# Attention and gated feed-forward on one core: one of two half-precision remainders moved from VectorE to GpSimd

## The chip, the cores and the metric

One core of a Trainium2 chip runs the whole program. The metric is the device time of one launch in microseconds (us); 1269.29 is the median of three runs before the change. The core has five engines with a queue of instructions each, worked off in order: TensorE (PE, whose weight loads appear as PEld), VectorE (DVE), ScalarE (ACT), GpSimd (POOL) and SyncE (SP, which only issues DMAs here).

## The reference

Block-causal attention over 8 batches of 8 heads, 576 positions, 64 dimensions, and behind it a feed-forward layer with a gate:

```python
scores = q @ k.T / 8                      # 64 x 64 blocks; a query sees its own and earlier blocks
attn = softmax(scores, masked)
x = (attn @ v) laid out as (8 * 576, 512)
h = x @ w_in                              # 512 -> 2048
out = (h * erf(softplus(h))) @ w_out      # 2048 -> 512
```

All inputs and outputs are 32-bit floats.

## The kernel before

Matrix products keep near 32-bit accuracy by splitting an operand into a high half in 16-bit floats and a low half, the remainder: `ph` is the rounded value, `pl` the value minus `ph`. A product is then three 16-bit matmuls (high x high, low x high, high x low).

**Attention.** A loop runs over the 64 heads `n`. In each turn the steps of several heads are merged: the loads of head n+3 (`load_qk`: two DMAs issued on GpSimd's queue, L383 and L385, one on SP's, then two GpSimd subtractions, L388 and L389, which make the low halves of keys and queries), the row maxima of head n+2 (`maxes`: matmuls L400, VectorE reductions L403 and L428), the probabilities of head n (`probs`) and, for every second n, the product with the values for heads n-2 and n-1 (`pv`: 42 matmuls of L495, then the row sums L518). Every fourth turn `normalise` scales two results and splits them (L578 on ScalarE, L579 on GpSimd) and stores them to DRAM (L580, issued on GpSimd's queue).

`probs` keeps the probabilities of one head in two column groups: part 0 with 832 columns, part 1 with 768. ScalarE writes exponentials (L451) into a 32-bit staging tile for each part (`p32_0`, `p32_1`, one buffer each). When a part is complete, `split` makes the two halves: ScalarE casts (L462), and an engine subtracts (L463). This happens for heads 24 to 63 only, thus 40 times for each part; the first 24 heads (batches 0 to 2) use the 32-bit values as they are. The last two steps of `probs` in a turn are the last two blocks of part 1, and `split(1)` behind them; so the low half of part 1 is made when the next turn has begun. For an odd head that turn is one that runs `pv`, whose 12th matmul is the first that reads the odd head's low half of part 1.

**Feed-forward.** In the same loop `moe1` feeds in units of the feed-forward layer on tokens whose attention is finished: 256 tokens by 256 of the 2048 features. A unit is 24 matmuls up (L190) into a PSUM bank `h`, of which there are two in the loop; the gate; and, three units later (`LAG = 3`), 12 matmuls down (L199). The gate is a chain that goes from engine to engine:

```python
# ScalarE L159, L160, L161: tanh of a scaled h, and two squares -> r0, r1 (SBUF)
nc.vector.scalar_tensor_tensor(out=r0, in0=r0, scalar=c3, in1=r0, op0=ALU.add, op1=ALU.mult)     # L162
nc.vector.scalar_tensor_tensor(out=r0, in0=r1, scalar=c4, in1=r0, op0=ALU.add, op1=ALU.mult)     # L163
nc.vector.scalar_tensor_tensor(out=r0, in0=r0, scalar=c5, in1=r0, op0=ALU.add, op1=ALU.mult)     # L164
nc.vector.scalar_tensor_tensor(out=r0, in0=r0, scalar=fin, in1=flat, op0=ALU.add, op1=ALU.mult)  # L165, flat is h in PSUM
nc.scalar.copy(gh, r0)                                                                            # L166
nc.gpsimd.tensor_tensor(out=gl, in0=r0, in1=gh, op=ALU.subtract)                                  # L167
```

After L165 the bank `h` is free for the unit after the next. When the heads are done, the remaining units run alone.

The order on each queue is set by a scheduler of the language, which replays the merged program with costs of its own and gives every engine its list; on the chip each list is worked off in order, and semaphores hold an instruction until its inputs are there.

Of the kernel before, what the change touches and what calls it, by code (L numbers as in the profile page):

```python
# [14 lines left out]
ALU = mybir.AluOpType  # L15
# [8 lines left out]
def f32(ap):  # L24
    return ap.bitcast(F32)
# [7 lines left out]
def tile_attention_moe(ctx: ExitStack, tc: tile.TileContext, qk, v, w, maskrows, sels, out):  # L33
    nc = tc.nc
# [259 lines left out]
    with tc.tile_pool(name="apool", bufs=2) as apool, tc.tile_pool(name="spool", bufs=1) as spool, \  # L294
# [14 lines left out]
        def bank(name):  # L309

            turn.append(0)
            k = len(turn) % 8 if not loaded else 0
            if k in (2, 5):
                return ps_h.tile([P, 512], F32, tag="h", name=name)
            if k in (3,):
                return ps_o.tile([P, 512], F32, tag="o", name=name)
            return ps_a.tile([P, 512], F32, tag="a", name=name)
# [55 lines left out]
        def part(n, i):  # L373

            return qks[n % NB][:, i * S : (i + 1) * S]
# [61 lines left out]
        def probs(n, out):  # L437

            K = D + 5
            klh, qhl, kh, qh = [part(n, i) for i in range(4)]  # L440

            def one(j, q0, w_, o):
                kk = min(P, S - j * P)
                ks = slice(j * P, j * P + kk)
                s = bank(f"t{j}_{n}_{q0}")
                nc.tensor.matmul(s[:kk, :w_], lhsT=kh[:K, ks], rhs=qh[:K, q0 : q0 + w_], start=True, stop=False)  # L446
                nc.tensor.matmul(s[:kk, :w_], lhsT=klh[:, ks], rhs=qhl[:, q0 : q0 + w_], start=False, stop=True)  # L447
                skip = max(0, starts[j] - q0)
                part, c = offs[j]
                c += q0 + skip - starts[j]  # L450
                nc.scalar.activation(p32s[part][:kk, c : c + w_ - skip], s[:kk, skip:w_], AF.Exp, scale=SCALE)  # L451

            pps = [apool.tile([P, 2, m], F16, tag=f"p{i}", name=f"p{i}_{n}", bufs=3) for i, m in enumerate(PN)]
            whole = n < B32 * H
            p32s = [f32(p.rearrange("p a b -> p (a b)")) for p in pps] if whole else pstage

            def split(part):
                if whole:
                    out.append((p32s[part],))
                    return  # L460
                ph, pl = pps[part][:, 0, :], pps[part][:, 1, :]
                nc.scalar.copy(ph, p32s[part])  # L462
                nc.vector.tensor_tensor(out=pl, in0=p32s[part], in1=ph, op=ALU.subtract)  # L463
                out.append((ph, pl))

            return [lambda: one(0, 0, 288, 0), lambda: one(0, 288, 288, 0), lambda: one(3, 320, 256, 0),
                    lambda: (one(4, 320, 256, 0), split(0)), lambda: one(1, 128, 448, 0),
                    lambda: (one(2, 256, 320, 0), split(1))]

        def pv(qd, pp, prs, V, usb, rs):  # L470
# [269 lines left out]
```

## Time and profile before

| | us |
|---|---|
| median of three runs (lowest, highest) | 1269.29 (1268.83, 1272.76) |
| the profiled execution | 1269.5 |
| its span, first to last instruction | 1267.5 |
| busy PE, DVE, ACT, POOL | 1174.1, 899.5, 778.0, 521.3 |
| L463 on VectorE, both parts: first and last start | 352.0, 1048.5 |
| L463, part 0 and part 1: busy | 44.2, 39.7 (40 instructions each) |

The page of the profile gives busy times of each engine, groups of instructions by source line with the idle time ahead of them and what ended it, and the chain of work that ended last. Matmuls are pipelined, and the busy time of PE contains this overlap. Beside the page stand answers of the trace for a stretch of time: the instructions in order with start and duration in us, and sums of what each engine waited for.

### The profile page before, as it was taken

The numbers are of one execution on the slowest core, as the hardware profiler recorded it, in microseconds if no ns is written. First come the engines' busy times: TensorE is split into PE (matmuls) and PEld (weight loads), VectorE is DVE, ScalarE is ACT, GpSimd is POOL, SyncE is SP. The second block draws the span as 40 slices with busy tenths as digits, with TensorE's granted clock in tenths as the row PEclk, the third lists the DMA queues.
The fourth block names the chain that finished last, engine by engine and source line by source line (L and its number), as shares of the span: only waits on it lengthen the run. The fifth ranks groups of instructions, "written<-read, shape, count | busy, mean of one in ns | idle before, by whom it ended". The sixth has DMA issues, their size and how long they took to land.

```text
span 1267.5 us, 23446 instructions
## 1 busy us (share of the span) xinstructions
PE 1174.1 (93%) x9018; PEld 812.4 (64%) x9018; DVE 899.5 (71%) x1601; ACT 778.0 (61%) x1555; POOL 521.3 (41%) x485
## 2 busy tenths in 40 slices
PE   5698798989999999999999999999999999999996
PEld 3465465566666666667667676766667766666563
DVE  4587698888677777887768777778777755464554
ACT  2465575667565666666666666665766765555543
POOL 6355454536443343545434453535444313212211
PEclk9777799999999999999999999999999999999999
DMA  9987568654444455354444554454444221121111
GB/s 235 221 211 191 140 186 196 168 131 114 111 120 112 120 120 126 98 141 118 100 115 117 122 124 116 116 125 118 109 126 116 58 68 58 54 83 35 59 58 50
DMA packets 95740, 151.72 MB, mean 120 GB/s; under 512 B 7738, under 2 KB 44922, under 8 KB 95630
## 3 DMA queue, kind: packets, MB, share of 16 engines
q1 hardware_dynamic: 69840, 93.34, 25.3%
q0 software_dynamic: 25120, 56.66, 22.2%
q8 instruction: 71, 1.16, 0.4%
q10 hardware_dynamic: 670, 0.23, 0.1%
q14 instruction: 39, 0.32, 0.1%
HBM read 121.66 MB, written 28.31 MB: 118 GB/s over the span
## 4 chain that ended last, share of the span: by engine, by line
PE 37%; DVE 30%; ACT 17%; DMA 8%; issue 5%; POOL 2%; ACTq 0%; DVEq 0%; SPq 0%; POOLq 0%
PE m_h L190 12%; PE o L199 11%; DVE m_r L163 6%; DVE m_r L162 5%; DVE m_r L164 5%; DVE m_r L165 4%; ACT m_r L159 4%; ACT m_r L160 4%; ACT m_r L161 4%; PE u L495 4%; DMA qk<-qk 2%; PE t L446 2%; DVE mx L403 2%; PE s L400 2%; DMA qk<-mt 2%
## 5 line engine op out<-in xcount | busy, mean ns | idle before, releaser
L190 PE MATMUL m_h<-xh,w 128*128 128x256 f16 x2304 | 477.2, 276 | 25.6 <-DVE m_r L165 18.5
L190 PEld LDWEIGHTS <-w 128*128 128x128 f16 x3456 | 328.0, 99 | 164.2 <-issue 33.7
L167 POOL TENSOR_TENSOR m_gl<-m_r,m_gh 128x512 f16<-128x512 f32 x144 | 175.6, 1220 | 423.5 <-ACT m_gh L166 365.2
L199 PE MATMUL o<-w,m_gh 128*128 128x512 f16 x1152 | 335.4, 383 | 12.2 <-DVE pt L240 8.6
L190 PE MATMUL m_h<-xl,w 128*128 128x256 f16 x1152 | 317.1, 275 | 0.3 <-DMA xl<-x_d 0.3
L162 DVE SCALAR_TENSOR_TENSOR m_r<-m_r 128x512 f32<-128x512 f32 x144 | 118.8, 825 | 189.8 <-ACT m_r L161 172.8
L403 DVE TENSOR_REDUCE mx<-s 64x1 f32<-64x288 f32 (+4 forms) x384 | 174.4, 469 | 83.8 <-PE s L400 82.6
L451 ACT ACTIVATE p<-t 128x288 f32<-128x288 f32 (+4 forms) x384 | 144.8, 384 | 99.5 <-PE t L447 89.0
L166 ACT CAST m_gh<-m_r 128x512 f16<-128x512 f32 x144 | 88.8, 617 | 188.6 <-DVE m_r L165 188.1
L199 PE MATMUL o<-w,m_gl 128*128 128x512 f16 x576 | 203.6, 383 | 0.3 <-POOL m_gl L167 0.3
L446 PE MATMUL t<-qk 69*128 69x288 f32 (+4 forms) x384 | 168.4, 439 | 11.2 <-DMA qk<-mt 8.0
L400 PE MATMUL s<-qk 68*64 68x288 f32 (+3 forms) x384 | 151.3, 425 | 27.0 <-DMA qk<-qk 21.9
L159 ACT ACTIVATE m_r<-m_h,c,bs 128x512 f32<-128x512 f32 (+3 forms) x192 | 124.3, 666 | 57.4 <-PE m_h L190 55.1
L388 POOL TENSOR_TENSOR qk<-st,qk 64x576 fp32r<-64x576 f32 x64 | 96.9, 1514 | 116.7 <-DMA qk<-qk 113.9
L199 PEld LDWEIGHTS <-m_gh 128*128 128x128 f16 x1152 | 100.5, 99 | 68.0 <-issue 17.3
L163 DVE SCALAR_TENSOR_TENSOR m_r<-m_r,m_r 128x512 f32<-128x512 f32 x144 | 121.0, 840 | 2.8
L447 PE MATMUL t<-qk 128*128 128x288 f32 (+4 forms) x384 | 120.4, 314 | 0.0
L164 DVE SCALAR_TENSOR_TENSOR m_r<-m_r 128x512 f32<-128x512 f32 x144 | 113.3, 787 | 2.4
L389 POOL TENSOR_TENSOR qk<-st,qk 64x576 fp32r<-64x576 f32 x64 | 99.3, 1552 | 35.9 <-DMA qk<-qk 28.1
L463 DVE TENSOR_TENSOR p<-p,p 128x832 f16<-128x832 f32 x80 | 84.0, 1050 | 34.8 <-ACT p L462 34.8
L161 ACT ACTIVATE m_r<-m_r,c 128x512 f32<-128x512 f32 x144 | 103.7, 720 | 2.8 <-ACT m_r L160 1.0
L160 ACT ACTIVATE m_r<-m_r,c 128x512 f32<-128x512 f32 x144 | 103.7, 720 | 1.7
(99 smaller groups left out, 1457.9 us busy)
## 6 DMA issues: line engine op xcount, KB each, us to landing
qk<-qk POOLq DMA_DIRECT2D x64, 432.0 KB, 5.0
st<-qk SPq DMA_DIRECT2D x64, 288.0 KB
qk<-qk POOLq DMA_DIRECT2D x64, 288.0 KB, 5.3
raw<-w SPq DMA_DIRECT2D x32, 512.0 KB
v<-v SPq DMA_DIRECT2D x16, 640.0 KB
x_d<-xs POOLq DMA_DIRECT2D x32, 288.0 KB, 3.9
xh<-x_d SPq DMA_DIRECT2D x36, 256.0 KB
xl<-x_d SPq DMA_DIRECT2D x36, 256.0 KB
```

What stands on the lines that cost most here:

```text
L159: nc.scalar.activation(r0s[:, :, lo:hi], h[:, :, lo:hi], AF.Tanh, bias=const(p1), scale=bss[b][g][:, 0:1])
L160: nc.scalar.activation(r1, r0, AF.Square, bias=const(b1), scale=a1)
L161: nc.scalar.activation(r0, r1, AF.Square, bias=const(b2), scale=a2)
L162: nc.vector.scalar_tensor_tensor(out=r0, in0=r0, scalar=c3, in1=r0, op0=ALU.add, op1=ALU.mult)
L163: nc.vector.scalar_tensor_tensor(out=r0, in0=r1, scalar=c4, in1=r0, op0=ALU.add, op1=ALU.mult)
L164: nc.vector.scalar_tensor_tensor(out=r0, in0=r0, scalar=c5, in1=r0, op0=ALU.add, op1=ALU.mult)
L167: nc.gpsimd.tensor_tensor(out=gl, in0=r0, in1=gh, op=ALU.subtract)
L190: nc.tensor.matmul(h[:, k, :], lhsT=wf[:, a, sl], rhs=x[:, cc, :], start=cc == 0 and i == 0, stop=cc == NCC - 1 and i == 2)
L199: nc.tensor.matmul(o[c], lhsT=a[:, sl], rhs=wf[:, b_, :], start=u == u0 and k == 0 and not lo and b_ == 2, stop=u == u1 - 1 and k == nu - ...
L400: nc.tensor.matmul(dst[:r, :w_], lhsT=qh[:K, i * P : i * P + r], rhs=kh[:K, k0 : k0 + w_], start=True, stop=True)
L403: nc.vector.tensor_reduce(out=mx[:r, col : col + 1], in_=src, axis=AX.X, op=ALU.max, negate=True)
L446: nc.tensor.matmul(s[:kk, :w_], lhsT=kh[:K, ks], rhs=qh[:K, q0 : q0 + w_], start=True, stop=False)
```

## The change

The remainder of part 1 (768 columns) is subtracted by GpSimd; that of part 0 (832 columns) stays on VectorE.

```diff
                 ph, pl = pps[part][:, 0, :], pps[part][:, 1, :]
                 nc.scalar.copy(ph, p32s[part])
-                nc.vector.tensor_tensor(out=pl, in0=p32s[part], in1=ph, op=ALU.subtract)
+                (nc.gpsimd if part else nc.vector).tensor_tensor(out=pl, in0=p32s[part], in1=ph, op=ALU.subtract)
                 out.append((ph, pl))
```

The scheduler also moves a few neighbours by one or two places. In the rows below, a name ends in a running number; `p_33` is the probabilities tile of head 33, `p_1` the staging tile of part 1, `m_4` a unit of the feed-forward layer, `mx` the maxima, `qk_126` to `qk_129` the four buffers of keys and queries.

GpSimd's queue at head 33, a head after which `pv` runs:

```order
 L580 DMA x_d<-xs_1_1_5968 128x2x576
 L383 DMA qk_127<-qk 64x3x576
-L385 DMA qk_127<-qk 64x2x576
 L167 TENSOR_TENSOR m_4_gl<-m_4_r_5952,m_4_gh 128x512
+L463 TENSOR_TENSOR p_33_5791<-p_1_140,p_33_5791 128x768
+L385 DMA qk_127<-qk 64x2x576
 L388 TENSOR_TENSOR qk_127<-st_6025,qk_127 64x576
 L389 TENSOR_TENSOR qk_127<-st_6025,qk_127 64x576
```

L463 stands behind the L167 of a gate, and the second DMA issue of the load, which stood ahead of that L167, now stands behind L463.

GpSimd's queue at head 25, where `normalise` also runs:

```order
 L167 TENSOR_TENSOR m_6_gl<-m_6_r_4036,m_6_gh 128x512
 L579 TENSOR_TENSOR xs_1_1_4069<-usb_3685,xs_1_1_4069 128x576
-L385 DMA qk_127<-qk 64x2x576
+L463 TENSOR_TENSOR p_25_3898<-p_1_140,p_25_3898 128x768
 L580 DMA x_d<-xs_1_1_4069 128x2x576
+L385 DMA qk_127<-qk 64x2x576
 L388 TENSOR_TENSOR qk_127<-st_4136,qk_127 64x576
```

Here L463 stands behind the L579 of `normalise`, ahead of its store and of the second DMA of the load.

VectorE's queue at head 47:

```order
 L163 SCALAR_TENSOR_TENSOR m_3_r_9256<-m_3_r_9257,m_3_r_9256 128x512
 L164 SCALAR_TENSOR_TENSOR m_3_r_9256<-m_3_r_9256 128x512
-L463 TENSOR_TENSOR p_47_9136<-p_1_140,p_47_9136 128x768
 L165 SCALAR_TENSOR_TENSOR m_3_r_9256<-m_3_r_9256,m_3_h 128x512
 L403 TENSOR_REDUCE mx_144<-s_50_9350 128x1 x2
```

L463 stood between the last two steps of a gate and is gone from there.

## The prediction, made before the change was run

> **What bounds the kernel now.** I read the page's busy line first, then the table by stretches, then the waits of each engine between 350 and 1060 us, because the edited line runs only there.
>
> ```profile
> PE 1174.1 (93%) x9018; PEld 812.4 (64%) x9018; DVE 899.5 (71%) x1601; ACT 778.0 (61%) x1555; POOL 521.3 (41%) x485
> ...
> 350.00:1060.00 710.00, 687.92 (x5719) 490.45 (x5719) 529.69 (x926) 469.12 (x919) 302.87 (x274) 1.00 0.45 111
> ...
> PE m_h L190 <- DVE m_r L165: 13.5, 15, 1.9
> PE o L199 <- DVE pt L240: 2.2, 2, 1.8
> ...
> PE u L495 <- DVE p L463: 0.6, 3, 0.2
> ...
> DVE p L463 <- ACT p L462: 34.8, 25, 4.4
> ```
>
> In the second row the figures after the length are PE, PEld, DVE, ACT and POOL busy. PE has work in 688 of 710 us at a granted clock of 1.00; VectorE in 530 (75%), GpSimd in 303 (43%). So PE is the resource that fills the stretch, and all that can be won is its 22 us of idle time. The waits say what it idles for: the largest is L165, the last VectorE step of a gate, which frees the PSUM bank that the next L190 matmuls need (15 times, 13.5 us). The low part of the probabilities (L463) holds up PE itself, in the L495 matmuls, for only 0.6 us. What VectorE loses elsewhere is hidden under PE. Nothing before 350 us or after 1060 us contains the edit.
>
> **The operation that moves.** In the same stretch, forms kept apart:
>
> ```profile
> L463 DVE TENSOR_TENSOR p<-p,p 128x768 f16<-128x768 f32 x40 | 39.7, 993 | 20.8 <-ACT p L462 20.8
> L167 POOL TENSOR_TENSOR m_gl<-m_r,m_gh 128x512 f16<-128x512 f32 x90 | 107.7, 1197 | 232.6 <-ACT m_gh L166 206.3 <-ACT p L451 15.6 <-issue 5.5
> L163 DVE SCALAR_TENSOR_TENSOR m_r<-m_r,m_r 128x512 f32<-128x512 f32 x89 | 78.8, 886 | 1.6
> L199 PEld LDWEIGHTS <-m_gl 128*128 128x128 f16 x360 | 33.8, 98 | 24.9 <-issue 4.7 <-POOL m_gl L167 0.2
> ...
> L163 DVE SCALAR_TENSOR_TENSOR m_r<-m_r,m_r x89: 670/691/2721, 355.0 to 1055.5; 128x512 f32<-128x512 f32 x89
> ...
> 379.34 1.27 POOL L579 TENSOR_TENSOR xs<-usb,xs 128x576 f16<-128x576 f32 x1
> ...
> 773.26 1.15 POOL L167 TENSOR_TENSOR m_gl<-m_r,m_gh 128x512 f16<-128x512 f32 x1 [3.73 <-ACT m_gh L166]
> ```
>
> The fifth row gives the shortest, median and longest L163; the last two, single instructions in order of time (start, duration). VectorE loses 40 instructions, 39.7 us, and 20.8 us in which its queue stood at one of them until ScalarE's cast (L462) was done. GpSimd gains the same 40. It has never run 768 columns, so I bound the price: L167, the same subtraction at 512 columns, takes 1.15 us undisturbed and L579 at 576 columns 1.27 us. The slope of these two gives 1.15 + 256 x 0.0019 = 1.63 us, plain scaling 1.15 x 768 / 512 = 1.73 us. I take 1.66, near the slope, since both rows carry a fixed part. That is 66 us on a queue with 407 us free: GpSimd does not become the bound.
>
> **Term 1: the consumer on PE.** For every second head the L495 group of 42 matmuls follows soon; its 12th matmul, 0.5 us after the start, is the first to read the low part of the odd head. Head 33:
>
> ```profile
> 520.07 0.83 ACT L462 CAST p<-p 128x768 f16<-128x768 f32 x1
> 521.89 0.69 DVE L164 SCALAR_TENSOR_TENSOR m_r<-m_r 128x512 f32<-128x512 f32 x1
> 522.50 0.95 DVE L463 TENSOR_TENSOR p<-p,p 128x768 f16<-128x768 f32 x1
> 523.36 0.68 DVE L165 SCALAR_TENSOR_TENSOR m_r<-m_r,m_h 128x512 f32<-128x512 f32 x1
> 524.10 0.27 PE L190 MATMUL m_h<-xh,w 128*128 128x256 f16 x1 [1.38 <-DVE m_r L165]
> 524.78 1.15 POOL L167 TENSOR_TENSOR m_gl<-m_r,m_gh 128x512 f16<-128x512 f32 x1 [2.19 <-ACT m_gh L166]
> 525.54 2.25 PE L495 MATMUL u<-p,v 128*64 128x256 f16 x42
> 526.18 0.69 DVE L162 SCALAR_TENSOR_TENSOR m_r<-m_r 128x512 f32<-128x512 f32 x1 [1.60 <-ACT m_r L161]
> 526.25 1.88 POOL L388 TENSOR_TENSOR qk<-st,qk 64x576 fp32r<-64x576 f32 x1 [0.32 <-DMA qk<-qk]
> 526.90 1.78 DVE L163 SCALAR_TENSOR_TENSOR m_r<-m_r,m_r 128x512 f32<-128x512 f32 x1
> ```
>
> The cast ends at 520.90, VectorE delivers at 523.45, PE asks at about 526.05. In the changed GpSimd queue L463 stands behind this very L167, which ends at 525.93; the low part is there at 525.93 + 1.66 = 527.59, so PE waits about 1.5 us. L165 comes up to 0.9 us earlier without L463 ahead of it, but that moves L167 and PE alike. Heads 25 and 57, the first and the last of the late ones:
>
> ```profile
> 380.87 2.25 PE L495 MATMUL u<-p,v 128*64 128x256 f16 x42
> ...
> 946.42 0.83 ACT L462 CAST p<-p 128x768 f16<-128x768 f32 x1
> 949.65 2.25 PE L495 MATMUL u<-p,v 128*64 128x256 f16 x42
> 949.76 0.75 POOL L580 DMA_DIRECT2D x_d<-xs  x1
> ```
>
> Head 25 stands behind the L579 of 379.34 (380.61 + 1.66 = 382.27, wanted at 381.4: 0.9 late), head 57 behind that L580 (950.51 + 1.66 = 952.17, wanted at 950.2: 2.0 late). Worked like this, 8 of the 20 odd heads come late (25, 29, 31, 33, 35, 37, 53, 57: 0.9, 1.1, 0.2, 1.5, 0.6, 0.1, 0.6, 2.0), together +7.0 us. The other twelve stand behind an L383 or L167 that is long done, and come in time. Bounds: 0, if PE takes it all back at later waits; +12.5, if each of the eight must also let one 0.69 us gate step pass (8 x 0.69 more), as told next.
>
> **Term 2: the gate chain.** The last three rows of head 33 show what two engines do to each other. L388 began during L162 and ended 1.26 us after it; L163 came during L388 and ended at 528.68, 0.55 us after L388's end at 528.13. Whoever comes second waits for the first: L163 took 1.78 where its median is 0.69. L165 reads PSUM (m_h) and has no such case. So an L463 on GpSimd no longer sits in VectorE's queue, but blocks an L162 to L164 that meets it. Head 47 shows the trade:
>
> ```profile
> 768.92 0.83 ACT L462 CAST p<-p 128x768 f16<-128x768 f32 x1
> 769.64 0.69 DVE L163 SCALAR_TENSOR_TENSOR m_r<-m_r,m_r 128x512 f32<-128x512 f32 x1
> 770.37 0.69 DVE L164 SCALAR_TENSOR_TENSOR m_r<-m_r 128x512 f32<-128x512 f32 x1
> 770.98 0.95 DVE L463 TENSOR_TENSOR p<-p,p 128x768 f16<-128x768 f32 x1
> 771.85 0.68 DVE L165 SCALAR_TENSOR_TENSOR m_r<-m_r,m_h 128x512 f32<-128x512 f32 x1
> 772.58 0.28 PE L190 MATMUL m_h<-xh,w 128*128 128x256 f16 x1 [1.22 <-DVE m_r L165]
> ```
>
> GpSimd would start at 769.8, wait for L163 until 770.33 and run to about 771.9; L164, ready at 770.35, ends 0.55 later (772.4) and L165 at 773.0 instead of 772.53: PE's wait grows by 0.5 us though 0.95 us left VectorE. Of the 15 L190 waits, seven have L463 in their chain. In three (451.7, 522.3, 1015.7) GpSimd comes after the chain: -0.8 each, -2.4. In four it meets L163 or L164: +0.55 each, +2.2. Outside L190 there are waits behind a VectorE queue that stood waiting for the cast, such as this one:
>
> ```profile
> 647.16 0.96 DVE L463 TENSOR_TENSOR p<-p,p 128x768 f16<-128x768 f32 x1 [1.62 <-ACT p L462]
> 650.00 1.25 PE L556 MATMUL rt<-sel,rs 128*128 128x4 f32 x10 [1.03 <-DVE mx L403]
> ```
>
> It goes (-1.0), and so does the longest L199 wait on L240, at 400.6, of the row at the top (-1.8): -2.8. Two more (506, 596) meet a blocked chain: +1.2. Eight chains for which PE did not wait also end about 0.6 us later; PE waits for 15 of 89 chains, a sixth, so +0.8 (bounds 0 and +4.8). Sum of term 2: -2.4 + 2.2 - 2.8 + 1.2 + 0.8 = -1.0. Its bounds are -5.2, if nothing is blocked, and +8.2, if nothing is won (2.2 + 1.2 + 4.8).
>
> **What I cost at nothing.** Behind L463 on GpSimd stand L385 (a DMA issue), L388, L389, an L580 and L167. The DMAs and L388/L389 prepare a head three loops ahead; the table of waits names no PE wait on them. L167 is covered by the three units of lag before its L199 matmuls, which wait 0.2 us in all for it (row above); a delay of 2 us fits, and if that cover were gone each unit would pay it on PE, 40 x 2 us at most. SP's queue keeps its rows but for swaps. The staging buffer that L463 reads is written again some 10 us later.
>
> **Sum.** +7.0 - 1.0 - 0.6 (the L495 waits that exist now) = +5.4 us on the profiled execution's 1269.5 us (span 1267.5 and 2.0 around it), which stands 0.2 above the median of the runs. That gives 1274.9; I forecast 1275.
>
> **Rivals.** *VectorE's relief wins (faster).* By one view VectorE drives the end:
>
> ```profile
> by line: PE m_h L190 14.7%; PE o L199 14.0%; DVE m_r L163 6.2%; DVE m_r L162 6.1%; issue 5.4%; DVE m_r L164 5.2%; ACT m_r L159 4.3%; DVE m_r L165 3.8%; ACT m_r L160 3.4%; DVE p L463 3.3%; ACT m_r L161 3.2%; PE u L495 2.9%; DVE mx L403 2.7%;
> ```
>
> In the chain of waits of this stretch L463 holds 3.3% of 710 us, 23 us, half of it ours. If the 60 us of work and waiting taken off VectorE take that half (11 us) off the end and the blocked chains give 3 back (2.2 + 0.8), the time is 1269.5 - 8 = 1261.5. It decides once the eight late heads cost under 2 us, for instance because ScalarE, freed sooner by L165, casts earlier. Against it: PE's 688 of 710. The Trainium skill, "Perfetto Trace Analysis", section "Identifying the Most-Contended Engine", would have PE judged by weight loads rather than by matmul busy time; by that rule 490 of 710 us (69%) puts PE behind VectorE's 75%, and this rival would be the forecast. Chance 0.25.
>
> *A draw.* The late heads are half taken back at the waits that follow: 5.4 - 3.5 = +1.9, 1271, within 0.3% (3.8 us, about what a measurement here tells from no change). For it: PE still idles 22 us at other places that can shrink. Against it: the waits named above mostly lie 15 us and more behind a late head. Chance 0.30.
>
> *The port decides (slower still).* If L463 meets a gate step in most heads, 30 x 0.55 us more on chains of which PE waits for half adds 8: 1283. L163's mean of 886 against its median of 691 ns says that today about one step in five is met (0.195 of the 1.09 us that head 33's cost), which speaks against it. The Trainium skill, "SBUF — State Buffer", section "Who interferes with whom", calls this an exclusive lock held for the whole instruction; the rows of heads 33 and 47 agree, and by that rule a longer GpSimd instruction blocks longer than L167 does now. Chance 0.10, beside 0.35 for the forecast.
>
> So slower 0.45, same 0.30, faster 0.25. The range goes from 1262 (nearly the first rival) to 1283 (the last). The forecast's own range is 1273.5 (the edge of the draw) to 1281 (the late heads at their upper bound, 12.5 instead of 7.0).
>
> **What would show it.** L463 on POOL at 1.63 to 1.73 us undisturbed; a new PE wait "u L495 on POOL p L463" of 5 to 9 us in 6 to 10 cases; L162 to L164 longer in the mean; the wait for L165 about as now; VectorE some 25 to 40 us less busy. The forecast is wrong if that L495 wait stays under 2 us, or if PE's other waits shrink by more than it.

## The result, and the profile after

The changed kernel is slower: 1313.45 us (median of 4 runs, 1309.61 to 1319.72) against 1270.05 us for the kernel before in the same session (4 runs, 1268.83 to 1272.76). The ratio is 1.033 with a 95% interval of 1.0293 to 1.0367. The forecast, 1275 us, had the sign and not the size, and the range ended at 1283. The sign, too, came from a term that the runs below show to be worth nothing measurable.

The profiled execution after took 1315.5 us (span 1313.7), 46.0 more than the one before. First the page's busy line of the changed kernel, and its line of granted PE clock in 40 slices:

```profile
PE 1196.4 (91%) x9018; PEld 823.8 (63%) x9018; DVE 900.1 (69%) x1561; ACT 776.9 (59%) x1555; POOL 582.7 (44%) x525
...
PEclk9776799899999899998999999999999999999999
```

VectorE has 40 instructions fewer and is as busy as before (900.1 against 899.5 us). PE has the same 9018 matmuls and is 22 us busier.

The table by stretches, cut where the edited line begins and some 10 us behind the start of its last instruction on part 0, which is 3 us behind the end of the last on part 1. Columns: length, then busy time of PE, PEld, DVE, ACT and POOL, then granted clock, DMA share, GB/s. The kernel before:

```profile
0.00:352.00 352.00, 298.13 (x2042) 198.50 (x2043) 261.49 (x520) 204.86 (x475) 175.11 (x173) 0.90 0.72 172
352.00:1053.00 701.00, 678.92 (x5632) 484.36 (x5631) 525.95 (x919) 463.63 (x909) 300.37 (x272) 1.00 0.45 112
1053.00:1267.00 214.00, 197.03 (x1348) 129.55 (x1345) 112.07 (x162) 109.49 (x173) 45.78 (x41) 0.99 0.18 58
```

The changed kernel:

```profile
0.00:358.00 358.00, 303.99 (x2042) 201.41 (x2043) 257.53 (x520) 204.67 (x475) 174.76 (x173) 0.88 0.71 169
358.00:1099.00 741.00, 696.38 (x5629) 493.30 (x5628) 530.48 (x879) 462.08 (x909) 361.40 (x312) 0.97 0.41 106
1099.00:1313.00 214.00, 196.02 (x1350) 129.06 (x1348) 112.11 (x162) 110.14 (x174) 46.58 (x41) 1.00 0.18 58
```

So 40 us were lost in the stage that contains the edit, 6 ahead of it, none behind it. The 40 split in two: PE's idle time grew from 22.1 (701.0 - 678.9) to 44.6 us, +22.5; its busy time grew by 17.5 us on the same matmuls, at a granted clock of 0.97 instead of 1.00. The 6 us are not the change's; they are taken up at the end.

Where the idle time comes from: the largest groups of PE's waits from 350 to 1107 us of the changed kernel (us in total, times, longest), then the same waits of the kernel before from 350 to 1060 us, as far as they are not shown above, and then VectorE's gate steps and GpSimd's L463 in the stage of the changed kernel:

```profile
PE m_h L190 <- DVE m_r L165: 21.2, 19, 3.0
PE u L495 <- POOL p L463: 6.4, 8, 1.4
PE rt L556 <- DVE mx L403: 3.9, 4, 1.8
PE mt L430 <- ACT p L451: 3.5, 4, 1.2
PE o L199 <- DVE pt L240: 2.8, 2, 2.1
PE t L446 <- DVE mx L403: 2.6, 2, 2.0
```

```profile
PE rt L556 <- DVE mx L403: 1.4, 2, 1.0
PE mt L430 <- ACT p L451: 0.7, 1, 0.7
...
PE t L446 <- DVE mx L403: 0.4, 1, 0.4
```

```profile
L163 DVE SCALAR_TENSOR_TENSOR m_r<-m_r,m_r 128x512 f32<-128x512 f32 x88 | 95.0, 1080 | 1.7
L162 DVE SCALAR_TENSOR_TENSOR m_r<-m_r 128x512 f32<-128x512 f32 x88 | 88.9, 1010 | 114.8 <-ACT m_r L161 98.7 <-ACT p L451 5.5 <-POOL p L463 5.2
L164 DVE SCALAR_TENSOR_TENSOR m_r<-m_r 128x512 f32<-128x512 f32 x88 | 75.9, 862 | 1.3
L463 POOL TENSOR_TENSOR p<-p,p 128x768 f16<-128x768 f32 x40 | 68.5, 1713 | 22.0 <-ACT p L462 21.7
```

The same three gate steps in the stage of the kernel before:

```profile
L163 DVE SCALAR_TENSOR_TENSOR m_r<-m_r,m_r 128x512 f32<-128x512 f32 x88 | 78.1, 888 | 1.5
L162 DVE SCALAR_TENSOR_TENSOR m_r<-m_r 128x512 f32<-128x512 f32 x88 | 75.0, 852 | 80.7 <-ACT m_r L161 67.6 <-ACT p L451 6.6 <-ACT mt L432 3.8
L164 DVE SCALAR_TENSOR_TENSOR m_r<-m_r 128x512 f32<-128x512 f32 x88 | 71.3, 810 | 1.0
```

The same 88 gates take 16.9 + 13.9 + 4.6 = 35.4 us more on VectorE, which gives back nearly all of the 39.7 us that were moved off it. One head shows how. The changed kernel at head 26, rows of VectorE, GpSimd and PE in order of time (start, duration; in brackets the idle time ahead and what ended it):

```profile
404.19 1.64 POOL L463 TENSOR_TENSOR p<-p,p 128x768 f16<-128x768 f32 x1 [1.40 <-ACT p L462]
...
404.83 1.55 DVE L162 SCALAR_TENSOR_TENSOR m_r<-m_r 128x512 f32<-128x512 f32 x1 [3.66 <-ACT m_r L161]
...
406.30 0.28 DVE L403 TENSOR_REDUCE mx<-s 128x1 f32<-128x128 f32 x1
406.43 1.41 POOL L388 TENSOR_TENSOR qk<-st,qk 64x576 fp32r<-64x576 f32 x1
406.50 1.89 DVE L163 SCALAR_TENSOR_TENSOR m_r<-m_r,m_r 128x512 f32<-128x512 f32 x1
...
408.32 0.41 DVE L403 TENSOR_REDUCE mx<-s 128x1 f32<-128x256 f32 x1
...
408.88 0.36 PE L446 MATMUL t<-qk 69*128 69x256 f32 x1 [1.96 <-DVE mx L403]
...
410.04 0.79 PE L199 MATMUL o<-w,m_gh 128*128 128x512 f16 x2 [0.69 <-DVE pt L240]
```

L162 starts during L463 and ends at 406.38, 0.55 us after L463's end at 405.83; L163 starts during L388 and ends 0.55 us after that. Each takes 1.55 and 1.89 us for a work of 0.69. A reduction of VectorE, L403, stands behind each, and PE waits 1.96 us for the second: a wait that has nothing to do with gate or probabilities except VectorE's queue.

What follows on PE is in the table by stretches of the same 14 us, in steps of 3.41 us:

```profile
403.50:406.90 3.40, 3.40 (x24) 2.16 (x21) 2.07 (x3) 2.19 (x5) 2.69 (x3) 1.00 0.59 129
406.90:410.31 3.41, 0.77 (x5) 0.54 (x5) 3.41 (x5) 0.00 (x0) 1.69 (x2) 1.00 0.40 87
410.31:413.72 3.41, 3.41 (x13) 1.90 (x12) 2.52 (x10) 3.07 (x7) 1.81 (x2) 0.50 0.68 217
413.72:417.14 3.42, 3.42 (x24) 2.30 (x22) 3.39 (x10) 2.27 (x4) 0.00 (x0) 1.00 0.33 105
```

PE was idle for 2.6 of 3.41 us, and in the next 3.41 us the granted clock is 0.50: PE is busy all the time with 13 matmuls where the steps around it hold 24. Then the clock is back. Such half-speed steps fill 41.0 us of the stage after and 6.8 us of the stage before; half of the difference is 17.1 us, the 17.5 us by which PE is busier.

### The profile page after: what moved, and what is told of

The parts are those of the page before. It is cut to its first block, busy times and chain, and to the rows that moved or that the text cites. A ratio compares the mean times of both kernels' runs of the same rounds, so it can differ in the third digit from the quotient of the medians.

```text
span 1313.7 us, 23456 instructions
## 1 busy us (share of the span) xinstructions
PE 1196.4 (91%) x9018; PEld 823.8 (63%) x9018; DVE 900.1 (69%) x1561; ACT 776.9 (59%) x1555; POOL 582.7 (44%) x525
## 4 chain that ended last, share of the span: by engine, by line
DVE 34%; PE 28%; ACT 20%; DMA 7%; issue 6%; POOL 4%; ACTq 0%; SPq 0%; DVEq 0%; POOLq 0%
PE m_h L190 8%; PE o L199 8%; DVE m_r L163 7%; DVE m_r L162 7%; DVE m_r L164 6%; DVE m_r L165 5%; ACT m_r L161 4%; ACT m_r L159 4%; ACT m_r L160 4%; PE u L495 3%; DMA qk<-qk 3%; DVE mx L403 3%; ACT m_gh L166 2%; PE t L446 2%; DVE p L463 2%
## 5 line engine op out<-in xcount | busy, mean ns | idle before, releaser
L190 PE MATMUL m_h<-xh,w 128*128 128x256 f16 x2304 | 484.5, 279 | 33.6 <-DVE m_r L165 25.6
L190 PEld LDWEIGHTS <-w 128*128 128x128 f16 x3456 | 331.4, 100 | 180.4 <-issue 42.4
L167 POOL TENSOR_TENSOR m_gl<-m_r,m_gh 128x512 f16<-128x512 f32 x144 | 171.6, 1192 | 415.0 <-ACT m_gh L166 342.4
L199 PE MATMUL o<-w,m_gh 128*128 128x512 f16 x1152 | 341.2, 388 | 14.0 <-DVE pt L240 9.2
L190 PE MATMUL m_h<-xl,w 128*128 128x256 f16 x1152 | 320.5, 278 | 5.0 <-DMA xl<-x_d 5.0
L162 DVE SCALAR_TENSOR_TENSOR m_r<-m_r 128x512 f32<-128x512 f32 x144 | 132.3, 919 | 229.1 <-ACT m_r L161 209.1
L403 DVE TENSOR_REDUCE mx<-s 64x1 f32<-64x288 f32 (+4 forms) x384 | 174.7, 469 | 102.7 <-PE s L400 101.8
L199 PE MATMUL o<-w,m_gl 128*128 128x512 f16 x576 | 204.9, 385 | 0.3 <-POOL m_gl L167 0.3
L451 ACT ACTIVATE p<-t 128x288 f32<-128x288 f32 (+4 forms) x384 | 144.8, 385 | 101.2 <-PE t L447 90.0
L446 PE MATMUL t<-qk 69*128 69x288 f32 (+4 forms) x384 | 170.5, 445 | 12.4 <-DVE mx L403 4.7
L199 PEld LDWEIGHTS <-m_gh 128*128 128x128 f16 x1152 | 101.5, 100 | 71.4 <-issue 18.8
L163 DVE SCALAR_TENSOR_TENSOR m_r<-m_r,m_r 128x512 f32<-128x512 f32 x144 | 136.0, 945 | 3.0
L388 POOL TENSOR_TENSOR qk<-st,qk 64x576 fp32r<-64x576 f32 x64 | 98.5, 1540 | 67.4 <-DMA qk<-qk 64.3
L164 DVE SCALAR_TENSOR_TENSOR m_r<-m_r 128x512 f32<-128x512 f32 x144 | 117.5, 816 | 2.7
L389 POOL TENSOR_TENSOR qk<-st,qk 64x576 fp32r<-64x576 f32 x64 | 96.1, 1501 | 48.7 <-DMA qk<-qk 44.8
L495 PE MATMUL u<-p,v 128*64 128x320 f16 (+9 forms) x1176 | 98.7, 316 | 7.0 <-POOL p L463 6.4
```

The costliest lines, as they stand in the source:

```text
L190: nc.tensor.matmul(h[:, k, :], lhsT=wf[:, a, sl], rhs=x[:, cc, :], start=cc == 0 and i == 0, stop=cc == NCC - 1 and i == 2)
L199: nc.tensor.matmul(o[c], lhsT=a[:, sl], rhs=wf[:, b_, :], start=u == u0 and k == 0 and not lo and b_ == 2, stop=u == u1 - 1 and k == nu - ...
L403: nc.vector.tensor_reduce(out=mx[:r, col : col + 1], in_=src, axis=AX.X, op=ALU.max, negate=True)
```

## The experiments

Three theories were on record with the first four runs. C, the consumer: the low part comes late at L495 (term 1). P, the port: a GpSimd subtraction blocks VectorE's two-operand steps, and PE waits for what is behind them. O, the order: the scheduler's moved rows cost the time, whatever engine subtracts. All runs, each beside the kernel before (medians 1270.15 to 1273.06 us in the sessions that followed); the sum of the mean durations of L162 to L164, the length of the stage (from the first L463 to some 10 us behind the start of the last one on part 0), and PE's busy and idle time in it, are from the table by stretches and the groups of the profiled execution:

| run | median us | ratio (95% interval) | L162+163+164 ns | stage us | PE busy | PE idle |
|---|---|---|---|---|---|---|
| before | 1270.05 | | 2550 | 701 | 678.9 | 22.1 |
| the change | 1313.45 | 1.033 (1.0293 to 1.0367) | 2952 | 741 | 696.4 | 44.6 |
| e1_late_use | 1311.43 | 1.0328 (1.025 to 1.0407) | 2945 | 740 | 695.1 | 44.9 |
| e7_late_use_before | 1266.26 | 0.9972 (0.9932 to 1.0012) | 2564 | 698 | 675.3 | 22.7 |
| e2_even | 1289.24 | 1.0152 (1.0061 to 1.0243) | 2717 | 713 | 683.2 | 29.8 |
| e8_odd | 1295.29 | 1.021 (1.0141 to 1.0279) | 2798 | 723 | 685.6 | 37.4 |
| e3_drop | 1265.93 | 0.9988 (0.995 to 1.0026) | 2543 | 692 | 674.8 | 17.2 |
| e4_extra | 1350.08 | 1.0633 (1.0544 to 1.0722) | 3107 | 774 | 703.6 | 70.4 |
| e6_memset | 1280.69 | 1.0102 (1.0065 to 1.014) | 2540 | 712 | 681.8 | 30.2 |
| e9_copy | 1334.95 | 1.0503 (1.0423 to 1.0582) | 2993 | 767 | 702.1 | 64.9 |
| e5_thirds | 1299.08 | 1.0233 (1.0152 to 1.0313) | 2840 | 727 | 686.9 | 40.1 |
| e10_qk_dve | 1258.22 | 0.9897 (0.9837 to 0.9957) | 2176 | 690 | 674.0 | 16.0 |
| e11_xs_dve | 1264.71 | 0.9963 (0.9928 to 0.9998) | 2476 | 698 | 677.4 | 20.6 |
| e13_change_qk_dve | 1286.19 | 1.0152 (1.0087 to 1.0216) | 2535 | 721 | 684.3 | 36.7 |
| e12_qk_xs_dve | 1254.85 | 0.9883 (0.9842 to 0.9925) | 2087 | 685 | 673.8 | 11.2 |

**The late low part, e1_late_use and e7_late_use_before.** The L495 products of the changed kernel in another order, those that read a low half last and part 1 behind part 0; and the same order in the kernel before as a control.

```diff
-                for j, kk, a, pt, cs in todo[j0:j1]:
-                    for iv, ip in terms:
...
+                todo = [(ip, ip * r[3], hf, iv) + r for hf, (q0, q1) in enumerate(halves) for r in ranges(q0, q1) for iv, ip in terms]
+                todo.sort(key=lambda o: o[:2])
```

> The changed kernel (1313 us), with the 42 matmuls of each L495 group in another order: all products with high parts first, then those with the low part of part 0, and those with the low part of part 1 last, so that the first one that needs GpSimd's L463 comes about 1.9 us after the group's start instead of 0.5. Theory C (the late low part at L495, 6.4 us of PE waits in the changed kernel, and the clock drops that follow them, make the loss): most of the 43 us goes, 1275 to 1285. Theory P (GpSimd's L463 blocks the gate steps L162 to L164) or theory O (the scheduler's new order on ScalarE and VectorE): only C's own share goes, 6 to 10 us, 1303 to 1308, and the mean of L162 to L164 stays near 0.98 us.

> The kernel before, with the L495 products in the order of the late-use run (the low part's products last). A control for that run: if the order costs nothing by itself, 1268 to 1274 us, and what the late-use run won against the changed kernel (about 2 us) is all that the late low part costs. If the order itself costs time, 1275 us or more, and the late low part was worth that much more than the late-use run showed.

One wait of L495 for GpSimd is left in the late-use run, of 0.5 us, so 5.9 of term 1's 6.4 us are gone; PE idles 44.9 us in the stage all the same, and the time is 2 us shorter, less than the measurement can tell. The order by itself costs nothing (0.9972, the interval holds 1). So the change costs the same 3% without the late low part. The wait at L495 was there and was worth nothing: PE spent it at other waits instead.

**Half of the heads, e2_even and e8_odd.**

```diff
+(nc.gpsimd if part and n % 2 == 0 else nc.vector).tensor_tensor(...)   # e2_even
+(nc.gpsimd if part and n % 2 else nc.vector).tensor_tensor(...)        # e8_odd
```

> Only the 20 even heads have L463 of part 1 on GpSimd; their low part is needed a whole turn later, so no L495 can wait for it. Theory C: back to the kernel before, 1270 to 1274. Theory P: half of the blocked gate steps stay, so about half of the loss less C's share, 1284 to 1294, with some 18 us more in L162 to L164 than before. Theory O (about half of the moved rows are there): 1280 to 1290 without longer L162 to L164.

> GpSimd subtracts in the odd heads alone, the other half of the run with the even heads. By the lock each head costs the same: half of the loss, 1287 to 1296 us, L162 to L164 near 2.75 us together. By late use only the odd heads matter, since the products over a pair of heads come directly behind the odd one's split: all of the loss that is due to it here, none with the even heads; with the even heads' 19 us on record that leaves 1294 us or more here, and waits of L495 for L463 of 6 us here against none there. The two differ in those waits rather than in the time.

The even heads, whose low part comes in time, cost 1.5%; the odd ones 2.1%, with the L495 wait (4.2 us in 6 cases). Together 3.6%, the whole of the change's 3.3% within the intervals. The loss goes by the subtraction, not by the consumer.

**The work left out, e3_drop.** The subtraction of part 1 is not made at all and the high half stands in its place as the low half; the order on PE, VectorE and ScalarE is that of the changed kernel.

```diff
-                nc.vector.tensor_tensor(out=pl, in0=p32s[part], in1=ph, op=ALU.subtract)
-                out.append((ph, pl))
+                part or nc.vector.tensor_tensor(out=pl, in0=p32s[part], in1=ph, op=ALU.subtract)
+                out.append((ph, ph if part else pl))
```

> The subtraction of part 1 is left out on every engine (the high part is used in its place, so the matmuls are the same in number). The orders of PE, VectorE and ScalarE are those of the changed kernel; GpSimd has its old load. Theory P or C: VectorE is relieved of 40 us and nothing is blocked, so not slower than before and perhaps 3 to 12 us faster, 1258 to 1268. Theory O: the new order itself costs, 1285 to 1310.

0.9988: the moved rows cost nothing, so O falls. And it bounds the prize: had the 40 instructions vanished from both engines, the kernel would have won too little to be measured.

**The work doubled, e4_extra.** The kernel before, with VectorE's subtraction kept and the same one made again by GpSimd into a buffer that nobody reads. PE, VectorE and ScalarE keep their order row for row.

```diff
+                part and nc.gpsimd.tensor_tensor(out=spare, in0=p32s[part], in1=ph, op=ALU.subtract)
```

> The kernel before, VectorE keeps every L463, and GpSimd makes the same subtraction of part 1 once more into a tile that nobody reads. The orders of PE, VectorE and ScalarE are those of the kernel before, so there is no new order and no late consumer. Theory P: L162 to L164 (and L463) grow by 30 to 45 us in sum and the kernel is 25 to 45 us slower, 1295 to 1315. Theories C and O: 1268 to 1274.

6.3% slower, beyond what any theory gave. Nobody waits for the extra result. The groups of its stage, and the wait of PE for VectorE's own L463:

```profile
L163 DVE SCALAR_TENSOR_TENSOR m_r<-m_r,m_r 128x512 f32<-128x512 f32 x88 | 98.4, 1118 | 1.5
...
L463 POOL TENSOR_TENSOR spare<-p,p 128x768 f16<-128x768 f32 x40 | 78.0, 1950 | 22.5 <-ACT p L462 22.0
...
L463 DVE TENSOR_TENSOR p<-p,p 128x768 f16<-128x768 f32 x40 | 50.4, 1260 | 21.4 <-ACT p L462 21.4
```

```profile
PE u L495 <- DVE p L463: 9.9, 8, 3.0
```

VectorE's own L463, released by the same cast, is blocked too (1260 instead of 993 ns) and comes late: L495 waits 9.9 us for it, where it was 0.6 in the kernel before. So a late low part has a place here, against my expectation, but as an effect of the blocking. VectorE also keeps its 40 instructions. These two are the likely reasons why this costs more than the change; no run separates them.

**Port or queue, e6_memset and e9_copy.** Two GpSimd instructions in each head beside VectorE's subtraction: writes of zeros, and copies.

```diff
+                part and [nc.gpsimd.memset(x, 0.0) for x in [spare] * 2]               # e6_memset, 1024 f32 a partition
+                part and [nc.gpsimd.tensor_copy(out=x, in_=ph) for x in [spare] * 2]   # e9_copy, 768 columns
```

> The kernel before, with VectorE's subtraction where it was and two GpSimd writes of zeros (1024 f32 a partition each, into a spare buffer) beside it in each of the 40 heads: GpSimd is as busy as with the subtraction or busier, but its added instructions read no SBUF operand. By the lock (two engines that read two SBUF operands each exclude one another): L162 to L164 stay near 850, 888 and 810 ns and the time is that of the kernel before, 1268 to 1276 us. By the queue (GpSimd's own later work, L167, L388 and L389, comes late behind the added instruction): as late as with the extra subtraction, 1310 to 1350 us, with waits of PE for GpSimd's low parts.

> The kernel before, with two GpSimd copies of the 768 columns into a spare buffer (one SBUF operand read, not two) in each of the 40 heads, at the place in GpSimd's order where the extra subtraction stood. The memsets of the earlier run were all issued between 241 and 389 us and so said little; these wait for the head's own p, as the subtraction did. By the lock, if two read operands are needed for it: L162, L163 and L164 stay near 850, 888 and 810 ns, and 1270 to 1282 us, since GpSimd is only busier. By the queue (L167, L388 and L389 late behind the added work): 1310 us or more, as with the extra subtraction, with the three operations not stretched. By a lock that any GpSimd instruction takes: the three stretched as with the extra subtraction, 1030, 1120 and 960 ns, and 1330 us or more.

The memsets wait for nothing and were all issued between 241 and 389 us, so the run misses its aim as a twin of e4_extra. It lost 1.0%, in a crowded GpSimd queue at that place (one wait of 7.8 us for L165). But it shows what a writing GpSimd does to VectorE; four memsets of 3.63 us in all and a gate beside them:

```profile
342.97 3.63 POOL L463 MEMSET spare<- 128x1024 f32 x4
343.33 0.69 DVE L162 SCALAR_TENSOR_TENSOR m_r<-m_r 128x512 f32<-128x512 f32 x1 [2.56 <-ACT m_r L161]
344.06 0.69 DVE L163 SCALAR_TENSOR_TENSOR m_r<-m_r,m_r 128x512 f32<-128x512 f32 x1
344.78 0.69 DVE L164 SCALAR_TENSOR_TENSOR m_r<-m_r 128x512 f32<-128x512 f32 x1
```

No step is stretched, and so it is wherever a gate step ran beside these memsets and no other GpSimd work: 25 steps of the run, each of 0.67 to 0.69 us. The copies stand where the extra subtraction stood, and read one operand. First the groups of the stage, then one gate step and the copy beside it:

```profile
L162 DVE SCALAR_TENSOR_TENSOR m_r<-m_r 128x512 f32<-128x512 f32 x88 | 88.5, 1006 | 85.2 <-ACT m_r L161 72.4 <-ACT p L451 6.5 <-ACT mt L432 3.8
L163 DVE SCALAR_TENSOR_TENSOR m_r<-m_r,m_r 128x512 f32<-128x512 f32 x88 | 88.3, 1004 | 1.5
L164 DVE SCALAR_TENSOR_TENSOR m_r<-m_r 128x512 f32<-128x512 f32 x88 | 86.5, 983 | 1.0
L463 POOL CAST spare<-p 128x768 f32<-128x768 f16 x80 | 81.3, 1016 | 23.0 <-ACT p L462 22.4
...
456.01 1.50 DVE L164 SCALAR_TENSOR_TENSOR m_r<-m_r 128x512 f32<-128x512 f32 x1
456.11 0.84 POOL L463 CAST spare<-p 128x768 f32<-128x768 f16 x1
```

All three steps are stretched, in sum nearly as with the extra subtraction (2993 ns against 3107, and 2550 without either); the L164 of the last rows ends 0.56 us behind the copy. Taken alone, this run and its time also fit a lock that any GpSimd instruction takes; the memsets speak against that one. So one read operand on GpSimd is enough; my expectation that it takes two was wrong. The queue theory, which had the three steps unstretched, falls, and none of PE's waits in this stage names a GpSimd instruction. The Trainium skill, "SBUF — State Buffer", section "Who interferes with whom", has it so: a VectorE instruction with two inputs in SBUF contends with a GpSimd instruction that reads SBUF, and not with one that only writes. Both runs agree (0.67 to 0.69 us beside memsets; with copies 0.98 to 1.01 in the mean of the stage, against 0.81 to 0.89 in the kernel before).

**Shorter instructions, e5_thirds.** The 768 columns on GpSimd in three instructions of 256.

```diff
+for c0, c1 in ((0, 256), (256, 512), (512, 768)): nc.gpsimd.tensor_tensor(out=pl[:, c0:c1], in0=p32s[part][:, c0:c1], in1=ph[:, c0:c1], op=ALU.subtract)
```

> The changed kernel, with each of GpSimd's 40 subtractions of 768 columns written as three of 256 columns. By length: if a VectorE gate operation has to wait for the end of one GpSimd instruction, and GpSimd's are now about 1.64 / 3 = 0.55 us plus some start-up, the longest wait falls from 1.6 to about 0.6 us, the mean sum of L162, L163 and L164 falls from 2.95 us to about 2.7 us, and the time to 1285 to 1300 us. By turns: if the two engines take turns, one instruction each, and a VectorE operation pays for every GpSimd instruction that comes between, three short ones block the gate's three operations as long as one long one blocks one: 2.9 us or more for the three, and 1310 to 1330 us. If the loss is only in when the low part is there (late use), 1313 us, since the last third ends no sooner.

1299.08 us and 2.84 us for the three steps: between the two accounts (2.7 and 2.9), the time inside the first's range. By the medians about a third of the loss goes (1.0233 against 1.033, with intervals that just overlap), which speaks for the length of the blocking instruction; the three together also take longer, some 0.67 us each, and whether turns are taken more often cannot be separated by this run.

**The reverse, e10_qk_dve and e11_xs_dve.** The kernel before, with other GpSimd subtractions moved to VectorE: L388 and L389, or L579.

```diff
-                nc.gpsimd.tensor_tensor(out=t[:D, 0, :], in0=st[:D, :], in1=f32(t[:D, 2, :]), op=ALU.subtract)
-                nc.gpsimd.tensor_tensor(out=t[D:, 1, :], in0=st[D:, :], in1=f32(t[D:, 1, :]), op=ALU.subtract)
+                nc.vector.tensor_tensor(out=t[:D, 0, :], in0=st[:D, :], in1=f32(t[:D, 2, :]), op=ALU.subtract)     # e10_qk_dve
+                nc.vector.tensor_tensor(out=t[D:, 1, :], in0=st[D:, :], in1=f32(t[D:, 1, :]), op=ALU.subtract)
...
-                nc.gpsimd.tensor_tensor(out=xs[:, 1, :], in0=x32, in1=xs[:, 0, :], op=ALU.subtract)
+                nc.vector.tensor_tensor(out=xs[:, 1, :], in0=x32, in1=xs[:, 0, :], op=ALU.subtract)                # e11_xs_dve
```

> The kernel before, with the two subtractions of each head's q and k (L388 and L389, 64 partitions by 576) on VectorE instead of GpSimd: the reverse of the change, at another place. GpSimd loses some 74 instructions of 1.45 us, 107 of its 242 us of two-operand work in the stage; VectorE gains 74 of an estimated 0.65 us, 48 us (from 685 ns for L577's and 679 for L165's like shapes). By the lock, L162 to L164 shorten from 2.55 us together to 2.25 to 2.35 us, and VectorE's busy time rises by 25 to 35 us instead of 48. The time: 1260 to 1270 us if VectorE's locked time counts alone; 1272 to 1290 us if VectorE, which takes its instructions in order, now waits for the loads behind L388.

> The kernel before, with the 20 subtractions of L579 (128 by 576, 1.35 us each on GpSimd) on VectorE, at an estimated 0.68 us each, 14 us. By the lock some 28 of GpSimd's 242 us of two-operand work go, and with them 4 to 6 us of the 42 us that L162 to L164 are stretched in the kernel before: VectorE's busy time rises by 8 to 10 us, and the time stays within 1262 to 1276 us. If taking GpSimd's work away at any place pays more than it costs, 1262 us or less.

More work on VectorE, and faster: 1.0% with L388 and L389, more than expected, and 0.4% with L579 (an interval that ends just below 1). With L388 and L389 moved, the three gate steps fall to 2176 ns, below the expected 2250. VectorE now waits at L388 and L389 for their loads (16.7 and 2.7 us from 350 to 1100 us), and PE idles less all the same (16.0 us in the stage against 22.1). One thing these runs leave open: the scheduler reorders far more here than for the change. Of VectorE's 1521 instructions other than the moved ones, some 230 left their old sequence in e10_qk_dve, 110 in e11_xs_dve and 270 in e12_qk_xs_dve, against some 40 for the change, and no run has the new order without the move, as e3_drop has it for the change.

**Both ways at once, e13_change_qk_dve and e12_qk_xs_dve.** The change together with L388 and L389 on VectorE; and the kernel before with L388, L389 and L579 on VectorE.

> The changed kernel (768 columns subtracted by GpSimd) with L388 and L389 on VectorE. GpSimd's work on SBUF operands in the stage is then about 136 + 68 = 204 us, below the 242 us of the kernel before. If the loss follows that total: L162 to L164 near 2.35 us together (between 2.18 and 2.55), and 1255 to 1268 us, faster than before. If it follows from where the subtraction stands, beside the gate chains: the change costs here as much as it cost by itself, 3%, or about two thirds of it, since 20 of its pairs now meet a less crowded GpSimd: 2.45 to 2.65 us together, and 1280 to 1297 us.

> The kernel before, with L388, L389 and L579 all on VectorE, so that in the stage GpSimd reads SBUF in L167 alone. The first two gave 0.990 of the time before and L579 alone 0.996. If the two add, 0.986, 1251 to 1258 us, with L162 to L164 at 2.1 us together (2.18 with the first two alone). If VectorE's queue is now the limit (it gains about 61 us and 17 us, less what it was locked out for), no better than the first two alone: 1257 to 1268 us, with more waits of PE for L165.

With the change on top, the gain of e10_qk_dve turns into a loss of 1.5%: 1.0152 / 0.9897 = 1.026, nearly the price of the change alone. GpSimd's total of subtractions is then lower than in the kernel before (203.5 against 242.5 us in the stage) and the gate steps are as long (2535 ns against 2550), yet PE idles 14.6 us more. So neither GpSimd's total nor the summed length of the gate steps sets the loss. What is left is where the steps are stretched: by the count described in the next section, 33.1 us of stretch lie beside the moved L463 here, and none beside L388 and L389, where the kernel before has 30.8. That the place behind the exponentials, beside the gates that PE waits for, is what costs is argued from this, not shown by a run that moves the place alone. And e12_qk_xs_dve is the fastest version: 1254.85 us, inside what was expected if the two gains add, 1.2% below the kernel before and, as a quotient of the two ratios, 4.3% below the changed one. The groups of its stage, and its waits of PE from 350 to 1100 us:

```profile
L162 DVE SCALAR_TENSOR_TENSOR m_r<-m_r 128x512 f32<-128x512 f32 x88 | 62.1, 705 | 41.0 <-ACT m_r L161 36.4 <-ACT p L451 4.0
L163 DVE SCALAR_TENSOR_TENSOR m_r<-m_r,m_r 128x512 f32<-128x512 f32 x88 | 61.6, 700 | 1.1
L164 DVE SCALAR_TENSOR_TENSOR m_r<-m_r 128x512 f32<-128x512 f32 x88 | 60.0, 682 | 0.8
...
L389 DVE TENSOR_TENSOR qk<-st,qk 64x576 fp32r<-64x576 f32 x36 | 32.2, 895 | 4.4 <-DMA qk<-qk 3.3
L388 DVE TENSOR_TENSOR qk<-st,qk 64x576 fp32r<-64x576 f32 x36 | 29.2, 812 | 10.8 <-DMA qk<-qk 10.8
```

```profile
PE m_h L190 <- DVE m_r L165: 9.2, 14, 1.7
```

The gate runs close to its undisturbed speed (0.685 us a step), and PE's largest wait has shrunk from 15.1 us (the same stretch before) to 9.2. Whether it differs from e10_qk_dve can't be said from the intervals.

## Why the prediction was wrong, point by point

- *The operation's price* (1.66 us, between 1.63 and 1.73): right. L463 on GpSimd takes 1.64 us undisturbed and 1.713 in the mean.
- *Term 1*, the late low part (+7.0 us in 8 heads): right as a wait, 6.4 us in 8 cases with a longest of 1.4, seven of them at the forecast heads (head 63 came in place of 37). Wrong as a term of the sum: e1_late_use takes 5.9 us of it away and wins nothing measurable. Its lower bound, zero because PE takes it back at later waits, was the value. The forecast had its sign from this term: without the +7.0 its sum is -1.6, faster than before. That the change came out slower, as forecast, was luck.
- *Term 2*, the gate chain (-1.0, bounds -5.2 and +8.2): this is the step that failed, on size: since term 1 is worth nothing, what stood at -1.0 is the stage's loss of some 40 us, 22.5 of it PE's idle time and 17.5 a lower clock. The mechanism was the one read from head 33 (the rows of head 47 hold no blocked step; the meeting there was worked out, not seen). Two things made it small. First, I priced a meeting at 0.55 us, the part of the gate step that runs on behind GpSimd's end, with the operation ready just before that end. Counted in the trace after, from the gate steps longer than 0.735 us that lie beside a GpSimd instruction (their time over 0.685 us, shared where there are two), 30 steps were stretched beside the moved L463, by 31.7 us: 1.06 us each; 26 of them end 0.55 us behind it. The steps beside L388 and L389 were stretched by 37.5 us, where it had been 30.8. Secondly, I let PE pay in the chains for which it already waited, and a sixth of the others. PE's idle time grew by 22.5 us: L190 waits 21.2 us instead of 13.5, where the prediction had the wait for L165 "about as now", but also L556, L446 and L199 wait longer, for reductions and accumulations that only share VectorE's queue with a stretched step. (L430's 3.5 us for ScalarE's L451, 0.7 before, were not followed further.)
- *A missing term*: the granted clock. No step of the prediction priced it, because it stood at 1.00 in the stage before. It made PE 17.5 us slower, nearly half of the 40.
- *The rival "the port decides"*, with a chance of 0.10, had the mechanism; its 30 meetings were the number that the count gives, and its 0.55 us, its half, and the missing clock made 8 us of what is 40.
- *VectorE 25 to 40 us less busy*: wrong. Over the whole run it is 0.6 us busier: it won 39.7 us of work and lost 35.4 us of it in L162 to L164.
- *The rival of VectorE's relief*: e3_drop shows that even the whole of the relief, with nothing given to GpSimd, isn't measurable. PE, not VectorE, was the bound.
- *At nothing* were L385, L388, L389, L580 and L167 behind L463: right as far as PE's waits name none of them after. L388 and L389 did block VectorE more than before, as told above, and that was not priced.

How the two parts of the loss hang together is an account, not an experiment: in all fifteen profiled executions the stage is 673 to 680 us plus PE's gaps of over 0.3 us between matmuls plus half of the time at half clock. No run held PE busy through a wait to keep the clock up.

Of the 46 us between the two profiled executions, 6 lie ahead of the edit: PE waits 4.7 us once at about 255 us for a load of `xl` in the execution after. A wait like it, of 5.3 us, stands in e7_late_use_before, where VectorE subtracts, and none in e3_drop. Two DMA queues issue within a microsecond there. What decides it stays open; since it comes without the change too, it isn't put down to it, and the runs of the kernel before alone spread over 1258.8 to 1279.35 us.

## What to carry to other kernels

Before work is moved from VectorE to GpSimd, look in the trace for VectorE's instructions with two operands in SBUF and ask which of them stand beside the moved one: here each GpSimd instruction that reads SBUF stopped a step that it met until it ended, so 68.5 us of GpSimd work took back 35.4 of the 39.7 us it relieved. Price a meeting by the stretch of such a step in the trace (here about 1 us), and count everything queued behind it, not only its chain. Where PE is the bound and waits for VectorE, the opposite move can pay: 1.2% here for some 79 us more work on VectorE, the scheduler's new order included.

## What the hardware showed that was not expected

The granted clock of PE falls in steps: in the stage every half-speed stretch lasts 3.41 us or a whole multiple of it. A half-speed step follows most often a step of 3.41 us in which PE was mostly idle, and no single long wait is needed: 1.96 and 0.69 us within one step did it. Counted over the stages of the fifteen executions, by the gaps between matmuls: all 22 full-speed steps that were idle for 64% or more were followed by a half-speed one, 27 of the 39 that were idle for 50 to 64%, and 16 of some 3000 that were idle for less. So idle time explains most of the half-speed steps and not all. A wait of 2.95 us for L165 that ended at 729.5 us in the changed kernel, spread over two such steps, lowered nothing (granted clock 1.00 from 720 to 735 us). Each half-speed step that PE fills costs 1.7 us of matmul work (half of 3.41), more than the mean wait at L190 (21.2 us in 19). The Trainium skill, "TensorE: Matmul & The Clock Gate", section "HAM oscillation — how this bites in real kernels", warns of idle gaps of PE above some 3.4 us; the rows at 406.90 and 410.31 show that shorter ones do it when they fall into one step.
